# Linear attention and a gated MLP on one core: 512-token chunks with a chunk of tails, block-diagonal kv, 1 KB loads, crossbar transposes of q, and a hand-made order

## The chip, the cores and the metric

The kernel runs on one core of a Trainium2 chip. The metric is the device time of one execution in microseconds (us); lower is better. The profile is one execution recorded by the hardware profiler. Its span runs from the first to the last recorded instruction and is a few us shorter than the timed execution. Engines are named as the profile names them: PE (matrix multiplier), PEld (its weight loads, which overlap PE), DVE (vector engine), ACT (activation engine), POOL (general engine), SP (here only the issuer of DMAs).

## The reference

Eight batches, eight heads, 576 tokens, head size 64. All inputs are float32.

```python
q_s = exp(q) / sum(exp(q), over the 64 features)    # the reference also subtracts maxima first
k_s = exp(k) / sum(exp(k), over the 576 tokens)
kv  = k_s^T v                    # 64 x 64 for each batch and head
x   = q_s kv                     # (8*576 = 4608 tokens) x 512, heads side by side
h   = x @ w_in                   # 512 -> 2048
g   = h * sigmoid(beta * h)
out = g @ w_out                  # 2048 -> 512
```

Both kernels use bfloat16 operands for the matmuls, leave the maxima out (the inputs are small), and get the sum over tokens for k from a column of ones appended to v. The MLP is the bulk: for each 512 tokens it takes 128 matmuls of 128x512 (64 into h, 64 into the output). For 4608 tokens that makes 1152.

## The kernel before

Tokens are cut in nine chunks of 512. A batch has 576 tokens, so each batch falls into two chunks, and into four blocks of 128 rows and one of 64. A scheduler chooses the order of instructions. The parts that matter, with cuts marked by `...`:

```python
S_CHUNKS = [(0, 128), (128, 128), (256, 128), (384, 128), (512, 64)]
...
qt = stage.tile([P, H, D], F32, tag="q_st", bufs=NSC)
nc.sync.dma_start(qt[:rows], q[b, :, s0 : s0 + rows, :].rearrange("h p d -> p h d"))     # 256 B runs
...
vt = atn.tile([P, H, D + 1], BF16, tag="vaug", bufs=ATN_DEEP)
nc.gpsimd.dma_start(vt[:rows, :, 0:D], v[b, ...])          # the DMA casts float32 to bfloat16
...
nc.vector.memset(vaug[ci][:rows, :, D : D + 1], 1.0)       # column of ones, again in every batch
...
for j in range(HP):                                        # two heads at a time
    for ci, (s0, rows) in enumerate(S_CHUNKS):             # four blocks of 128 rows, one of 64
        nc.tensor.matmul(kvE[:, :], Ek[ci][:rows, ds(P * j, P)], vaug[ci][:rows]..., ...)
    ...
    for ci, (s0, rows) in enumerate(S_CHUNKS):
        nc.tensor.transpose(qsT_ps[:, s0 : s0 + rows], qs[ci][:rows]..., identity[:rows, :rows])
    ...
    # x: two 64x64 matmuls side by side, one head each
    nc.tensor.matmul(xps[0:D, 0:w], kvp[0:D, :], qsT[0:D, ...], tile_position=(0, 0))
    nc.tensor.matmul(xps[D:P, 0:w], kvp[D:P, :], qsT[D:P, ...], tile_position=(64, 64))
    nc.scalar.copy(xT[c][:, j, off : off + w], xps[:, 0:w])
```

The MLP comes in two passes per chunk: all of h and g (`mlp_A`), then the output (`mlp_B`, one chunk behind).

The softmax here doesn't subtract the row's maximum and nothing guards it: scores larger than these inputs give would overflow.

## Time and profile before

| | before |
|---|---|
| time, first three runs | 370.23 us median (369.5 to 370.23) |
| span of the profiled run | 366.7 us |
| first MLP weight load starts at | 34.2 us |
| 129th (a chunk's worth later) | 87.5 us |
| 257th | 123.2 us |
| 1152nd, the last | 362.1 us |

The weight loads of the MLP's matmuls are a good ruler: there are exactly 1152 in both kernels, so the n-th one marks the same progress, whatever the order. Back to back, 128 of the matmuls take 27.6 us (0.2157 us from one start to the next), so a chunk cannot be shorter than that.

First, the page of the kernel before: its span, PE's busy line, and three rows in 40 slices of the span (granted PE clock in tenths of full speed, DMA share in tenths, GB/s).

```profile
span 366.7 us, 4552 instructions
...
PE 317.5 (87%) x1570; PEld 139.3 (38%) x1600; DVE 207.0 (56%) x477; ACT 185.2 (50%) x325; POOL 69.3 (19%) x86
...
PEclk9999768999999999999999999999999999999999
DMA  8999999649719802950293019001001000100111
GB/s 187 250 356 327 266 254 241 160 103 219 204 46 188 221 31 78 182 150 27 62 179 115 2 57 93 30 0 57 27 3 57 32 29 2 57 29 29 59 67 76
```

PE is busy 87% of the time. In the first seven slices (64 us) the DMA engines are nearly full, but move only 187 to 356 GB/s. The granted clock is known only from the first clock record of a trace on, at 37.8 us in the kernel before; the views count the time ahead of it as full speed. Next, PE's waits over the whole run, with the instruction that ended each (total us, times, longest us).

```profile
PE qsT_ps L179 <- DVE qst L137: 17.8, 5, 9.8
PE hT L213 <- DVE g L225: 12.9, 11, 3.4
PE kvE L157 <- DVE vt L127: 7.2, 3, 3.3
```

The first line is mostly the start: q has to be loaded, exponentiated and normalized before it can be transposed. The third is the ones column: `vt L127` is the memset. The stretches view gives for each stretch its length, the busy time of PE, PEld, DVE, ACT and POOL with counts, then the granted clock, the DMA share (the summed times of all packets over 16 engines, so it can exceed 1), and GB/s.

```profile
34.20:87.50 53.30, 44.36 (x203) 17.84 (x206) 38.21 (x94) 31.22 (x60) 18.68 (x22) 0.87 1.15 205
...
160.80:198.30 37.50, 35.50 (x182) 15.68 (x185) 23.83 (x57) 21.20 (x39) 8.44 (x10) 1.00 0.51 93
```

The first chunk's worth of MLP work took 53.3 us, a later one 37.5 us, in which PE counts as busy for 35.5. In the first, the granted clock fell twice to one half for 6.8 us, and 27 of the 128 MLP matmuls took about 0.63 us each instead of 0.38. Busy isn't the same as useful: the timeline of PE shows how a 64-row block sits among the others (start, us, engine, line, operation, operands, size of the weights, size of the result).

```profile
251.94 0.39 PE L157 MATMUL kvE<-vt,Ekt 128*128 128x130 bf16 x4
252.26 0.24 PE L193 MATMUL xps<-qsT,kvp 64*64 64x128 bf16 x1
252.26 0.24 PE L199 MATMUL xps<-qsT,kvp 64*64 64x128 bf16 x1
252.43 0.23 PE L157 MATMUL kvE<-vt,Ekt 64*128 64x130 bf16 x1
252.59 0.40 PE L179 MATMUL qsT_ps<-identity,qst 128*128 128x128 bf16 x4
```

From the start of the 64x64 pair to that of the 64x128 matmul it is 0.17 us, and 0.16 us more until the next 128x128 one may start. Matmuls of this size and equal tiles start 0.057 us apart in the same trace. The Trainium skill, "TensorEngine Tiling (Array Packing)", "Key Properties", says: "Changing tiling mode (not just tile) drains the TensorE". The trace agrees, and shows the price.

### The profile page before, as it was taken

How to read it: one execution, taken by the hardware profiler on the slowest of the kernel's cores; microseconds unless marked ns; L12 is line 12 of the kernel's file. 1: busy time of each engine (PE TensorE's matmuls, PEld its weight loads, DVE VectorE, ACT ScalarE, POOL GpSimd, SP SyncE). 2: the span in 40 equal slices, each digit the busy share in tenths (PEclk: the TensorE clock that was granted, in tenths of full speed). 3: DMA queues.
4: the chain of work that ended last, by engine and by line, in shares of the span. 5: the costliest groups of instructions: out<-in, count | busy, mean ns of one | idle time of the engine just before them, and what ended most of it. 6: DMA issues, size and time to landing. Idle time of an engine off the chain costs nothing.

```text
span 366.7 us, 4552 instructions
## 1 busy us (share of the span) xinstructions
PE 317.5 (87%) x1570; PEld 139.3 (38%) x1600; DVE 207.0 (56%) x477; ACT 185.2 (50%) x325; POOL 69.3 (19%) x86
## 2 busy tenths in 40 slices
PE   0125669899998999899989998999999999999995
PEld 0011223443433444344433443345344444444442
DVE  1554736988988937664767566654452545255100
ACT  3312426768668745755485538552554355355211
POOL 8281433035017001800090004000000000000000
PEclk9999768999999999999999999999999999999999
DMA  8999999649719802950293019001001000100111
GB/s 187 250 356 327 266 254 241 160 103 219 204 46 188 221 31 78 182 150 27 62 179 115 2 57 93 30 0 57 27 3 57 32 29 2 57 29 29 59 67 76
DMA packets 88486, 41.72 MB, mean 114 GB/s; under 512 B 78480, under 2 KB 78480, under 8 KB 88464
## 3 DMA queue, kind: packets, MB, share of 16 engines
q0 software_dynamic: 40448, 14.16, 28.8%
q1 hardware_dynamic: 48016, 27.28, 26.3%
q8 instruction: 12, 0.20, 0.2%
q14 instruction: 10, 0.08, 0.1%
HBM read 36.71 MB, written 9.44 MB: 126 GB/s over the span
## 4 chain that ended last, share of the span: by engine, by line
PE 67%; DMA 12%; DVE 11%; issue 4%; ACT 3%; SPq 2%; POOL 1%; ACTq 0%; POOLq 0%
PE hT L213 30%; PE acc L241 27%; DMA qt<-in_q_dram 6%; DMA vt<-in_v_dram 4%; PE kvE L157 4%; PE qsT_ps L179 3%; DVE g L225 3%; PE xps L193 3%; DMA w_in_st_311<-in_moe_w_in_dram 3%; DVE qst L137 2%; SPq L109 2%; DVE qz L131 2%; ACT th L221 1%; DVE w_in_b L86 1%; DVE qsT L185 1%
## 5 line engine op out<-in xcount | busy, mean ns | idle before, releaser
L241 PE MATMUL acc<-w_out_b,g 128*128 128x512 bf16 x561 | 143.8, 381 | 0.6 <-DVE g L225 0.2
L221 ACT ACTIVATE th<-hT,beta_half 128x512 bf16<-128x512 f32 x144 | 97.8, 686 | 72.4 <-PE hT L213 68.8
L225 DVE SCALAR_TENSOR_TENSOR g<-th,hT 128x512 bf16<-128x512 bf16 x144 | 97.7, 685 | 64.8 <-ACT th L221 64.4
L213 PEld LDWEIGHTS <-w_in_b 128*128 128x128 bf16 x576 | 54.4, 98 | 87.3 <-issue 34.4
L241 PEld LDWEIGHTS <-g 128*128 128x128 bf16 x576 | 54.9, 98 | 63.8 <-issue 0.9
L121 POOL DMA_DIRECT2D vt<-in_v_dram x40 | 33.9, 871 | 121.6 <-DVE qz L131 101.8
L249 ACT COPY o_sb<-acc 128x512 f32<-128x512 f32 x36 | 21.0, 584 | 44.6 <-PE acc L241 41.1
L179 PE MATMUL qsT_ps<-identity,qst 128*128 128x128 bf16 (+1 forms) x160 | 18.8, 226 | 19.1 <-DVE qst L137 17.8
L131 DVE TENSOR_REDUCE qz<-Eq 128x8 f32<-128x512 bf16 (+1 forms) x40 | 26.8, 671 | 13.3 <-ACT Eq L129 8.7
L129 ACT ACTIVATE Eq<-qt 128x512 bf16<-128x512 f32 (+1 forms) x40 | 25.0, 627 | 11.0 <-DMA qt<-in_q_dram 8.5
L137 DVE TENSOR_TENSOR qst<-Eq,rqz 128x512 bf16<-128x512 bf16 (+1 forms) x40 | 27.1, 684 | 2.6 <-DVE rqz L135 1.9
L157 PE MATMUL kvE<-vt,Ekt 128*128 128x130 bf16 (+1 forms) x160 | 20.9, 232 | 7.8 <-DVE vt L127 7.2
L213 PE MATMUL hT<-xT_93,w_in_b 128*128 128x512 bf16 x63 | 20.7, 469 | 6.0 <-DVE g L225 5.8
L193 PE MATMUL xps<-qsT,kvp 64*64 64x512 bf16 (+7 forms) x64 | 20.2, 316 | 3.9 <-DVE kvp L170 2.6
L179 PEld LDWEIGHTS <-qst 128*128 128x128 bf16 (+1 forms) x160 | 11.1, 99 | 27.3 <-DVE qst L137 19.6
L199 PE MATMUL xps<-qsT,kvp 64*64 64x512 bf16 (+7 forms) x64 | 20.3, 317 | 0.3 <-issue 0.3
L167 DVE RECIPROCAL rkz<-kvE 64x1 f32<-64x1 f32 x32 | 5.0, 158 | 27.3 <-PE kvE L157 26.5
L157 PEld LDWEIGHTS <-Ekt 128*128 128x128 bf16 (+1 forms) x160 | 12.4, 100 | 19.6 <-issue 10.7
L213 PE MATMUL hT<-xT_96,w_in_b 128*128 128x512 bf16 x63 | 16.4, 378 | 2.0 <-DVE g L225 2.0
L213 PE MATMUL hT<-xT_97,w_in_b 128*128 128x512 bf16 x63 | 16.5, 378 | 1.6 <-DVE g L225 1.6
L213 PE MATMUL hT<-xT_94,w_in_b 128*128 128x512 bf16 x62 | 16.4, 380 | 0.9 <-DVE g L225 0.8
L213 PE MATMUL hT<-xT_95,w_in_b 128*128 128x512 bf16 x62 | 16.2, 379 | 1.1 <-DVE g L225 0.9
(121 smaller groups left out, 222.7 us busy)
## 6 DMA issues: line engine op xcount, KB each, us to landing
out_dram<-o_sb SPq DMA_DIRECT2D x36, 256.0 KB, 2.0
qt<-in_q_dram SPq DMA_DIRECT2D x32, 256.0 KB, 5.4
vt<-in_v_dram POOLq DMA_DIRECT2D x32, 128.0 KB, 5.6
qt<-in_q_dram SPq DMA_DIRECT2D x8, 128.0 KB, 6.1
w_out_st_315<-in_moe_w_out_dram SPq DMA_DIRECT2D x1, 1024.0 KB, 12.0
w_out_st_317<-in_moe_w_out_dram SPq DMA_DIRECT2D x1, 1024.0 KB, 14.9
w_out_st_319<-in_moe_w_out_dram SPq DMA_DIRECT2D x1, 1024.0 KB, 10.7
w_out_st_321<-in_moe_w_out_dram SPq DMA_DIRECT2D x1, 1024.0 KB, 11.8
```

The lines of the kernel that those rows point to most:

```text
L121: nc.gpsimd.dma_start(vt[:rows, :, 0:D], v[b, :, s0 : s0 + rows, :].rearrange("h p d -> p h d"))
L129: nc.scalar.activation(Eq[:rows], q_st[ci][:rows], ACTF.Exp)
L131: nc.vector.tensor_reduce(qz[:rows], Eq[:rows], axis=mybir.AxisListType.X, op=ALU.add)
L137: nc.vector.tensor_tensor(qst[:rows], Eq[:rows], rqz[:rows].unsqueeze(2).to_broadcast((rows, H, D)), ALU.mult,)
L157: nc.tensor.matmul(kvE[:, :], Ek[ci][:rows, ds(P * j, P)], vaug[ci][:rows].rearrange("p h e -> p (h e)")[:rows, ds(2 * j * (D + 1), 2 * (D ...
L179: nc.tensor.transpose(qsT_ps[:, s0 : s0 + rows], qs[ci][:rows].rearrange("p h d -> p (h d)")[:rows, ds(j * P, P)], identity[:rows, :rows],)
L193: nc.tensor.matmul(xps[0:D, 0:w], kvp[0:D, :], qsT[0:D, s_done : s_done + w], tile_position=(0, 0),)
L213: nc.tensor.matmul(hT[:, :], w_in_b[:, kt, ds(j * P, P)], xT[c][:, kt, :], start=(kt == 0), stop=(kt == KT - 1),)
L221: nc.scalar.activation(th[:, :], hT[:, :], ACTF.Tanh, scale=beta_half[:, j : j + 1])
L225: nc.vector.scalar_tensor_tensor(out=g[:, :], in0=th[:, :], scalar=1.0, in1=hT[:, :], op0=ALU.add, op1=ALU.mult,)
L241: nc.tensor.matmul(acc[:, :], gts[j][:, ds(st * P, P)], w_out_b[:, j, :], start=(j == 0), stop=(j == NJ - 1),)
L249: nc.scalar.copy(o_sb[:, :], acc[:, :])
```

## The change

Its intent: cut each batch into 512 tokens, which make a chunk on their own, and 64 tails, which make a ninth chunk together (8 x 64 = 512). Give each SBUF partition four consecutive tokens, so that a load has 1 KB runs. Make every matmul a full 128x128 tile: the tails of two batches share 128 rows, with zeros in v where the rows belong to the other batch; kv of two heads is one block-diagonal matrix with zeros off the diagonal. Let the DMA's crossbar transpose q from batch 1 on. Write the ones columns once (as 2.0, which also absorbs the factor one half of the tanh form). Interleave the two MLP passes two units apart, with four accumulators, and fix the order of the instructions by hand. POOL casts most of v and w_out.

The diff, cut to its core (cuts marked by `...`):

```diff
-    S_CHUNKS = [(0, 128), (128, 128), (256, 128), (384, 128), (512, 64)]
+    MAIN = R * P            # 512
+    TAIL = S - MAIN         # 64
...
+    ctx.enter_context(tc.manual_schedule())
...
-            nc.sync.dma_start(
-                qt[:rows], q[b, :, s0 : s0 + rows, :].rearrange("h p d -> p h d")
-            )
+    def main_view(t, b):
+        return t[b, :, 0:MAIN, :].rearrange("h (p i) d -> p h (i d)", i=R)
...
-            nc.gpsimd.dma_start(
-                vt[:rows, :, 0:D], v[b, :, s0 : s0 + rows, :].rearrange("h p d -> p h d")
-            )
...
-            nc.vector.memset(vaug[ci][:rows, :, D : D + 1], 1.0)
+    nc.gpsimd.memset(va[0][:, :, :, D:D1], 2.0)        # once; the same for va[1] and the tails
...
-                nc.tensor.transpose(
-                    qsT_ps[:, s0 : s0 + rows],
...
+        nc.sync.dma_start_transpose(
+            qsT[b][:].rearrange("p i j r -> p (i j) r"),
+            qs[b][:].rearrange("p i h d -> p (i h d)"),
+        )
...
-                nc.tensor.matmul(xps[0:D, 0:w], kvp[0:D, :], qsT[0:D, ...], tile_position=(0, 0))
-                nc.tensor.matmul(xps[D:P, 0:w], kvp[D:P, :], qsT[D:P, ...], tile_position=(64, 64))
+            nc.tensor.matmul(t[:], kvp[:, c, j, :], qsT[c][:, :, j, :])
...
+    WARM = 36
+    for wi in range(WARM):                             # dummy matmuls while the first loads arrive
+        t = ps.tile([P, 512], F32, tag="h", bufs=2, name=f"warm{wi}")
+        nc.tensor.matmul(t[:], warm[:, 0:P], warm[:])
...
+    nc.gpsimd.memset(kvp[:, 1:B], 0.0)                 # after the first chunk's x, in program order
+    nc.gpsimd.memset(vt[:, 1:4], 0.0)
...
+            off = {0: "q0", 1: "q1", 2: "k0", 3: "k1", 5: "qT", 7: "kv0", 9: "kv1"}   # unit of the chunk
```

The last line is the hand-made order of a chunk: in which of its 16 MLP units the exponentials and sums of the next batch's q, its k, the transpose and kv are issued. This is called side work below.

## The prediction

> **What bounds it now.** The span is 366.7 us. The chain of waits is 67% PE, 12% DMA, 11% DVE. In steady state (timeline after 300 us) four 128x512 matmuls take 0.86 us, so the MLP's 1152 cost about 248 us. Attention on PE costs roughly 40 us: transposes about 92 ns each (x160), kv matmuls about 96 ns (x160), the paired x matmuls about 10 us in all. The other 75 us are idle or slow PE. By the stretches table PE is busy 4.0 of the first 30 us (q and k arrive in 256 B packets; the first MLP matmul starts at 34.2 us), and from 30 to 87 us it stalls for weights and loads (waits of PE: transposes on qst 17.8 us, hT on g 12.9 us) at a granted clock of 0.87 to 0.90. After 115 us PE is over 94% busy.
>
> **What the change does.**
> 1. Start. q0, k0, v0 and one weight block (4.4 MB) must land. The 1 KB loads should reach about the 320-350 GB/s that the best slice of before reaches, so the first block lands near 17.5 us; cast (1.3 us, as the 128x2048 DVE cast now), kv norm and x copies follow. First MLP matmul near 21.5 us: 12-13 us saved.
> 2. Chunk 0. All weights and batch 1 (about 15 MB) stream to 46-50 us, while 16 units of 1.73 us need only 28 us of PE. POOL now casts w_out and v (2048 elements); the trace shows no POOL copy, my estimate is 4-5 us each, from the "GPSIMD Engine Reference", section 3.1, of the Trainium skill (2.6 cycles an element). Its page "SBUF — State Buffer", "Who interferes with whom", says a DVE cast of this kind and POOL exclude each other, so some DVE casts will wait: no view of before shows it. Chunk 1 starts near 58 us, with 5-8 us of PE stall.
> 3. Steady chunks 1-6: 27.6 us MLP + 1.9 kv + 0.9 x. Seven batches' PE transposes (12 us) leave. A new loss: in the first four units of each chunk DVE owes two row sums (1.2 us for 1024 elements, scaled from 0.68 for 512), two normalizations (1.2), two output copies (0.6) and four g (0.69): near 10 us against 7 us of PE. With two h buffers and single output accumulators, I expect 2 us of PE stall a chunk: 32.5 us each, 195 us together. The crossbar transpose (512 KB) has about 9 us before x needs it; I expect it hidden.
> 4. Chunk 7 about 31.5 us, chunk 8 about 28 us, drain and last store 5 us.
>
> Sum: 58+195+31.5+28+5 = 318 us span; the timed runs are 3.5 us above the span: 321 us. I shade to 318, as the order was presumably tuned.
>
> **Prediction: 318 us, range 302 to 336.** Faster by over 2%: 0.98; within 2%: 0.015; slower: 0.005. The gain, all on the critical path: 13 us start, 15 us PE transposes and x, 20 us stalls between 34 and 115 us.
>
> **What would show it.** First hT matmul 19-24 us; chunk-1 start 54-63 us; PE's waits, before the first matmul of a chunk's second or third unit, on output copies (accumulators) and on g; no PE wait on the transposed q; DMA mostly over 300 GB/s in the first 40 us.
>
> **What would make it wrong.** A slow crossbar transpose, or one that stops other loads (then x waits in each chunk: up to 5 us x 7); POOL casts much slower than estimated, delaying w_out and v in chunk 0; the 4-byte beta load just ahead of the first weight block; or stalls at chunk starts absent (then about 304 us).

## The result and the profile after

| | before | after |
|---|---|---|
| time, median of 4 runs | 369.88 us (369.5 to 370.23) | 316.22 us (314.24 to 316.92) |
| ratio | | 0.8546 (95%: 0.8513 to 0.858) |
| span, profiled run | 366.7 us | 314.3 us |
| mean granted clock (time without a record counted as full) | 0.980 | 0.975 |

A ratio is the mean time of one kernel's runs over the mean of the other's in the same rounds, so it is not quite the ratio of the medians quoted. Executions over 1.5% slower than the fastest of the same kernel are left out of the means. Where two variants are compared that ran in different rounds, I divide their ratios to the kernel before, and multiply by 316.22 us to get microseconds against the changed kernel.

The same parts of the page, after:

```profile
span 314.3 us, 3735 instructions
...
PE 281.7 (90%) x1401; PEld 131.0 (42%) x1428; DVE 189.2 (60%) x292; ACT 153.9 (49%) x220; POOL 40.8 (13%) x41
...
PEclk9958999999999999999999999999999999999996
DMA  7989999995903692379039923870380033012005
GB/s 247 188 295 372 307 347 260 308 285 102 349 18 133 151 293 92 133 166 304 0 134 189 261 88 136 232 235 2 133 184 19 0 146 55 2 42 91 2 0 133
```

PE's waits after, and then two of its stretches:

```profile
PE kv_0_246 L218 <- DVE va_73 L147: 6.2, 1, 6.2
PE tp_2_226 L201 <- DVE qs_207 L182: 3.3, 1, 3.3
...
PE kv_0_515 L218 <- POOL va_74 L147: 1.1, 1, 1.1
...
PE acc_1_1213 L291 <- DVE o_1190 L250: 0.7, 1, 0.7
```

```profile
26.40:62.30 35.90, 31.04 (x148) 13.72 (x152) 22.54 (x34) 17.06 (x25) 8.39 (x5) 1.00 1.08 316
...
125.50:156.20 30.70, 29.80 (x151) 14.01 (x153) 19.55 (x32) 17.21 (x26) 2.10 (x2) 1.00 0.51 154
```

The longest waits for loads and for g are gone. What stays are waits in the start (6.2 and 3.3 us), single ones of up to 1.6 us in the first two chunks, and 0.7 us at the start of each later chunk. In the first chunk the DMA moves 316 GB/s where it moved 205. A later chunk takes 30.7 us instead of 37.5. And the timeline of PE shows kv, tails included, as full tiles that start 0.055 to 0.06 us apart:

```profile
55.23 0.39 PE L218 MATMUL kv_0_515<-va_74,ek_485 128*128 128x130 bf16 x4 [1.09 <-POOL va_74 L147]
55.45 0.22 PE L225 MATMUL kv_0_515<-vt,ekt 128*128 128x130 bf16 x1
55.51 0.39 PE L218 MATMUL kv_0_515<-va_74,ek_485 128*128 128x130 bf16 x4
```

By the ruler of MLP weight loads, the 52.4 us of span divide so:

| stretch | before | after | gain |
|---|---|---|---|
| until the first load | 34.2 | 26.4 | 7.8 |
| 1st to 129th | 53.3 | 35.9 | 17.4 |
| 129th to 257th | 35.7 | 32.5 | 3.2 |
| 257th to the last | 238.9 | 211.0 | 27.9 |
| from the last to the end | 4.6 | 8.5 | -3.9 |

So there are two things to explain: some 28 us in the first chunks, and some 28 us in the steady part. The latter isn't spread evenly: from the 257th load on, the seven pieces of 128 loads (127 in the last) gained 6.9, 6.8, 6.5, 4.5, 4.3, -0.8 and -0.2 us. For the first three of these pieces I took the time that PE spends on each kind of matmul, from the start of each matmul to that of the next. The figure for waits is what remains of the period.

| us for one chunk | before | after |
|---|---|---|
| MLP matmuls, back to back | 27.6 | 27.6 |
| kv | 2.0 | 1.1 |
| transposes of q | 2.1 | 0 |
| x | 2.4 | 0.9 |
| all other waits of PE | 3.4 | 1.1 |
| period | 37.5 | 30.7 |

Of the 6.8 us, 4.5 to 4.6 are matmuls that became cheaper or left, and 2.2 to 2.3 are waits. In the next two pieces PE of the kernel before waits only 0.2 us in all, so the gain there, 4.5 and 4.3 us, can't come from shorter waits. That is bookkeeping; whether each part would have been a gain alone, the experiments tell.

### The profile page after: what moved, and what is told of

It reads as the page before. It is cut to its first block, busy times and chain, and to the rows that moved or that the text cites. A ratio compares the mean times of both kernels' runs of the same rounds, so it can differ in the third digit from the quotient of the medians.

```text
span 314.3 us, 3735 instructions
## 1 busy us (share of the span) xinstructions
PE 281.7 (90%) x1401; PEld 131.0 (42%) x1428; DVE 189.2 (60%) x292; ACT 153.9 (49%) x220; POOL 40.8 (13%) x41
## 4 chain that ended last, share of the span: by engine, by line
PE 71%; DVE 15%; DMA 4%; ACT 4%; issue 3%; POOL 1%; another core or an unknown queue 1%; DVEq 0%; SPq 0%; ACTq 0%; POOLq 0%
DMA v_st_127<-in_v_dram 4%; DVE va_73 L147 2%; PE acc_1_2625 L291 1%; DVE w_in_b L125 1%; PE acc_3_2363 L291 1%; PE acc_2_2362 L291 1%; PE acc_0_2624 L291 1%; PE acc_2_2626 L291 1%; PE acc_2_1214 L291 1%; PE acc_1_2361 L291 1%; PE acc_1_1790 L291 1%; PE acc_1_1498 L291 1%; PE acc_1_2075 L291 1%; PE acc_3_1215 L291 1%; PE acc_0_2360 L291 1%
## 5 line engine op out<-in xcount | busy, mean ns | idle before, releaser
L343 PEld LDWEIGHTS <-warm 128*128 128x128 bf16 x36 | 3.8, 108 | 6.8 <-issue 2.4
L147 DVE CAST va_73<-v_st_101 128x1024 bf16<-128x1024 f32 x2 | 6.3, 3178 | 0.0
L147 POOL CAST va_73<-v_st_998 128x2048 bf16<-128x2048 f32 x1 | 1.9, 1917 | 32.5 <-DMA v_st_998<-in_v_dram 32.5
L147 POOL CAST va_73<-v_st_1575 128x2048 bf16<-128x2048 f32 x1 | 1.9, 1917 | 32.4 <-DMA v_st_1575<-in_v_dram 32.4
L174 DVE TENSOR_REDUCE rq_204<-eq_202 128x16 f32<-128x1024 bf16 x2 | 2.4, 1214 | 5.6 <-ACT eq_202 L161 5.6
L255 PEld LDWEIGHTS <-kvp 128*128 128x128 bf16 x32 | 3.0, 99 | 5.4 <-DVE kvp L239 2.1
L147 POOL CAST va_74<-v_st_1285 128x2048 bf16<-128x2048 f32 x1 | 1.9, 1918 | 24.3 <-DMA v_st_1285<-in_v_dram 24.3
L147 POOL CAST va_74<-v_st_1862 128x2048 bf16<-128x2048 f32 x1 | 1.9, 1918 | 23.5 <-PE x_2_1978 L255 23.5
L182 DVE TENSOR_TENSOR qs_643<-eq_595,rq_597 128x1024 bf16<-128x1024 bf16 x2 | 4.1, 2072 | 0.0
L131 ACT ACTIVATE ek_238<-k_st_94 128x1024 bf16<-128x1024 f32 x2 | 2.1, 1056 | 3.5 <-DMA k_st_94<-in_k_dram 3.5
L147 POOL CAST va_74<-v_st_708 128x2048 bf16<-128x2048 f32 x1 | 1.9, 1919 | 14.3 <-PE x_2_824 L255 14.3
L147 POOL CAST va_73<-v_st_580 128x2048 bf16<-128x2048 f32 x1 | 1.9, 1917 | 13.4 <-DMA v_st_580<-in_v_dram 13.4
L155 POOL CAST vt<-vt_st_99 64x512 bf16<-64x512 f32 x2 | 2.3, 1152 | 9.8 <-DMA vt_st_99<-in_v_dram 9.7
L161 ACT ACTIVATE eq_202<-q_st_91 128x1024 bf16<-128x1024 f32 x2 | 2.1, 1056 | 2.9 <-DMA q_st_91<-in_q_dram 2.9
L225 PEld LDWEIGHTS <-ekt 128*128 128x128 bf16 x32 | 3.3, 104 | 0.0
L155 POOL CAST vt<-vt_st_577 64x512 bf16<-64x512 f32 x2 | 3.3, 1638 | 0.1
L125 POOL CAST w_out_b<-w_out_117 128x2048 bf16<-128x2048 f32 x1 | 2.1, 2072 | 8.7 <-DMA w_out_117<-in_moe_w_out_dram 8.7
```

Source lines behind the costliest of these rows:

```text
L125: eng.tensor_copy(dst, wst[kind, blk][:])
L131: nc.scalar.activation(ek[b][:, :, s * m : (s + 1) * m, :].rearrange("p i h d -> p h i d"), k_st[b][:, s * m : (s + 1) * m, :].rearrange(" ...
L147: eng.tensor_copy(va[b % 2][:, :, s * m : (s + 1) * m, 0:D].rearrange("p i h d -> p h i d"), v_st[b][:, s * m : (s + 1) * m, :].rearrange( ...
L155: eng.tensor_copy(vt[r, pr, e, :, 0:D], vt_st[pr][r])
L174: nc.vector.tensor_reduce(rq[b][:, 0, :, h], eq[b][:, :, h, :], axis=AX.X, op=ALU.add)
L182: nc.vector.tensor_tensor(qs[b][:, :, h, :], eq[b][:, :, h, :], rq[b][:, 1, :, h].unsqueeze(3).to_broadcast((P, R, m, D)), ALU.mult,)
```

## The experiments

Theory at the outset: the steady part gains because PE does less (no transposes, no switches of tile size), and the early part gains because the loads are faster. The rivals: the hand-made order makes most of the gain; or the dummy matmuls keep the clock up; or the crossbar transposes are the main thing. Seven runs undo or move one part of the changed kernel, three put parts of the change into the kernel before, and two try to beat both.

### The steady part, from the changed kernel

**The crossbar.** All transposes back on PE, with DVE copying the results out:

```diff
-XBAR = True
+XBAR = False
```

> Undoes the crossbar: q of batches 1 to 7 and of the tails is transposed on PE again (16 transposes and four DVE copies of 0.42 us a batch). Theory A (the gain is mostly stalls removed by order and loads): transposes go at about 55 ns each in the changed kernel (four from 10.91 to 11.13 us), so 8 x 16 x 55 ns = 7 us more PE work, total +5 to +9 us (about 322 us). Theory B (the gain is PE work removed, as before spent 92 ns on each): +12 us or more (328 us or more). If PE had slack: under +2 us.

Measured: 321.02 us median (319.88 to 323.25), ratio 0.8678, so 0.8678/0.8546 = 1.015, or 4.9 us more. A steady chunk took 31.6 us instead of 30.7. Six of the seven batches fall after the 257th weight load, and that stretch grew by 5.4 us, from 211.0 to 216.4 (6 x 0.9). The crossbar is worth about 5 us, not the 12 us that the prediction charged for seven batches of PE transposes. With full tiles a transpose on PE is cheap. The crossbar itself is hidden. Its line in the changed kernel's timeline is:

```profile
165.52 1.95 SPq L191 DMA_TRANSPOSE qsT_1550<-qs_1505  x1
```

The view of that source line gives 4.3, 4.4 and 9.4 us (least, median, most) from issue to landing for 512 KB, the longest in the first chunk, where the loads are dense. No wait of PE names the transposed q. The Trainium skill, "Advanced Engine Details and Errata", "X-Bar Transpose (TRN2)", calls these transposes as fast as regular DMAs, at 350-400 GB/s. Here 512 KB in 4.4 us is about 120 GB/s (524,288 bytes divided by 4.4 us), counted from issue to landing; the issuing instruction on SP alone took 1.3 to 2.0 us of it after the first chunk, and plain stores of 512 KB took 3.2 us at the median. So for one transpose at a time, plan with the measured 4.4 us and not with the rate; one size can't tell how much of it is a fixed latency.

**Tile switches.** The x matmul of the changed kernel as two 64x64 ones again, on the same data:

```diff
-            nc.tensor.matmul(t[:], kvp[:, c, j, :], qsT[c][:, :, j, :])
+            for e in range(2):
+                r = slice(e * D, (e + 1) * D)
+                nc.tensor.matmul(t[r, :], kvp[r, c, j, r], qsT[c][r, :, j, :], tile_position=(e * D, e * D))
```

> Undoes the block-diagonal kv in the x matmuls of batches 0 to 7: two 64x64 matmuls on opposite quarters of the array, as before, in place of one 128x128. Theory C (a weight load of another tile size is not loaded ahead: in before the array drained at each switch, 149 ns from the last full kv matmul to the 64-row one and 155 ns to the next full one, against 57 ns between equal tiles): about 0.2 us a pair, 32 pairs, total +5 to +8 us, and a gap before and after each pair. Rival (the two quadrants run at once, so they cost what one matmul does): under +1 us.

Measured: 322.06 us (320.71 to 322.6), ratio 0.8734: 2.2%, or 7.0 us, more. The period rose from 30.7 to 31.6 us, 0.9 us for four pairs, 0.22 us for each. PE's timeline of this run shows it:

```profile
144.84 1.03 PE L293 MATMUL acc<-w_out_b,g 128*128 128x512 bf16 x4
145.79 0.40 PE L257 MATMUL x<-qsT,kvp 64*64 64x512 bf16 x2
146.13 1.03 PE L271 MATMUL h<-xT,w_in_b 128*128 128x512 bf16 x4
```

And the same place in the changed kernel:

```profile
146.88 0.38 PE L291 MATMUL acc_3_1215<-w_out_b,g_9_1335 128*128 128x512 bf16 x1
147.10 0.38 PE L255 MATMUL x_1_1385<-qsT_1266,kvp 128*128 128x512 bf16 x1
147.31 1.03 PE L269 MATMUL h_12_1388<-xT_80,w_in_b 128*128 128x512 bf16 x4
```

A full tile with half of its weights zero costs 0.21 us, start to start. The pair, which does half of that tile's multiplications, and in parallel, costs 0.34 us, and about 0.09 us before it (four matmuls from 144.84 at 0.2157 us would end their slots at 145.70). So zeros are cheaper than a switch. The rival, that a pair running in parallel costs the same as one full tile, falls.

**The hand-made order.** The same program with the scheduler's order:

```diff
-    ctx.enter_context(tc.manual_schedule())
```

> Undoes the hand-made order alone: same instructions, the order on each engine is left to the scheduler. Theory A: the order is worth a large part, +10 to +30 us, with PE gaps in the first 100 us and chunk periods above 30.7 us. Rival (the gain is less work and better loads, whatever the order): under +5 us.

Measured: 312.42 us (311.45 to 314.24), ratio 0.8444. That is 3.8 us faster than the changed kernel, where 10 to 30 us slower had been expected. My expectation was refuted, and with it the rival that the order makes the gain. What the change gained, it gained by its structure, and the order that was fixed by hand was even slightly worse than the scheduler's for the same program. By the ruler the scheduler's order is behind at first (385th load at 127.3 us, 125.5 by hand), and its chunks then take 30.5 us, falling to 29.6, against 30.7.

### The early part, from the changed kernel

**POOL and DVE locking each other out.** In the timeline of the changed kernel, all engines, the start looks like this:

```profile
15.17 3.08 POOL L364 MEMSET kvp<- 128x3584 bf16 x1
...
15.93 6.28 DVE L147 CAST va_73<-v_st_101 128x1024 bf16<-128x1024 f32 x2
...
18.25 2.77 POOL L366 MEMSET vt<- 128x3120 bf16 x1
...
22.12 1.23 DVE L125 CAST w_in_b<-w_in_105 128x2048 bf16<-128x2048 f32 x1
```

Two casts of 1024 elements take 6.28 us, where one of 2048 elements takes 1.23 us. They span POOL's two large memsets. The Trainium skill, "SBUF — State Buffer", "Who interferes with whom", says that a DVE cast in its fast mode and a POOL instruction need the same pair of ports, and whichever starts first blocks the other fully. The test moves POOL's memsets to before the first batch's work:

```diff
+    nc.gpsimd.memset(kvp[:, 1:B], 0.0)
+    nc.gpsimd.memset(va[1][:, :, :, D:D1], 2.0)
+    nc.gpsimd.memset(vt[:, 1:4], 0.0)          # and the small ones that follow it
     nc.gpsimd.memset(kvp[:, 0], 0.0)
     for wi in range(WARM):
...
-    nc.gpsimd.memset(kvp[:, 1:B], 0.0)
-    nc.gpsimd.memset(va[1][:, :, :, D:D1], 2.0)
-    nc.gpsimd.memset(vt[:, 1:4], 0.0)
```

> The POOL memsets of kvp, va and vt move ahead of POOL's wait for the v tail. If they are what made the two DVE casts of v take 3.2 us each (15.9 to 22.2 us), the casts fall to about 0.7 us each; if the casts waited for something else, they stay. Then the first MLP matmul comes 1.5 to 5 us earlier (22 to 25 us, limited by the landing of the first weight block near 20.6). Total: if the DMA stream (last load of batch 1 landing at 53 us) sets the start of chunk 1, the total changes by under 1.5 us; if the start sets it, by 4 to 5 us.

Measured: 315.39 us (314.43 to 316.86), ratio 0.8523; against 0.8546 that is no difference that the intervals can tell. The timeline of this run:

```profile
3.71 3.13 POOL L341 MEMSET kvp<- 128x3584 bf16 x1
...
16.80 1.29 DVE L147 CAST va<-v_st 128x1024 bf16<-128x1024 f32 x2
...
21.55 1.23 DVE L125 CAST w_in_b<-w_in 128x2048 bf16<-128x2048 f32 x1 [3.46 <-DMA w_in<-in_moe_w_in_dram]
```

POOL's memsets did hold up the casts: the mean cast went from 3178 to 690 ns. But the first MLP weight load came only 0.5 us sooner (25.9 us), because DVE then waits 3.46 us for the first weight block, which landed at 21.5 us (20.6 in the changed kernel). One wait was hiding another that ended at about the same time. A difference of 0.5 us between two single traces is no gain that counts: in the runs with PE transposes and with 64x64 pairs, which leave the loads and casts of the start as they are, the first load came at 25.7 and 25.0 us.

**The dummy matmuls.**

```diff
-WARM = 36
+WARM = 0
```

> Takes the 36 dummy matmuls away. They end at 10.9 us, PE then idles from 15.5 to 21.7 us and the granted clock falls to 0.5 before the first kv matmul, so theory A: nothing is gained by them, total within 1 us of the changed kernel, clock in the stretch 16 to 26 us unchanged. Rival (they keep PE fast for the start): the eight to ten transposes and the first MLP matmuls run at half clock, +2 us or more.

Measured: 315.0 us (314.64 to 315.64), ratio 0.8539. The dummies are worth nothing that these runs can see. The idea behind them agrees with the Trainium skill, "TensorE: Matmul & The Clock Gate", "Part 1: The HAM clock gate", which says that PE's clock is halved after an idle window of some 3.4 us and that activity releases it. For 16 to 26 us the stretches view gives a granted clock of 0.53 with the dummies and 1.00 without them, but the second is no measurement: the clock records of that trace begin at 24.6 us, and the time ahead of them counts as full. The matmuls tell more. First without the dummies, then with them:

```profile
8.49 1.03 PE L201 MATMUL tp<-identity,qs 128*128 128x128 bf16 x8 [8.49 <-DVE qs L182]
...
20.97 0.64 PE L218 MATMUL kv<-va,ek 128*128 128x130 bf16 x4
```

```profile
10.91 0.39 PE L201 MATMUL tp_0_210<-identity,qs_207 128*128 128x128 bf16 x4
...
22.22 0.64 PE L218 MATMUL kv_0_246<-va_73,ek_238 128*128 128x130 bf16 x4
```

The transposes start 107 ns apart without the dummies and 55 to 56 ns apart right after them. But the dummies end long before the real work starts, PE then stands idle for the 6.2 us shown above, and from the second kv matmul on they start 107 to 111 ns apart in both runs: half speed, as the records with the dummies show (0.5 from 15.2 to 25.4 us). What the dummies had won was lost before it mattered, as I had expected.

**The length of the runs in the loads.** Each main load in four pieces with 256 B runs, to the same places:

```diff
-            eng.dma_start(t[:, s * n : (s + 1) * n, :], main_view(src, b)[:, s * n : (s + 1) * n, :])
+            for i in range(R):
+                eng.dma_start(
+                    t[:, s * n : (s + 1) * n, i * D : (i + 1) * D],
+                    main_view(src, b)[:, s * n : (s + 1) * n, i * D : (i + 1) * D],
+                )
```

> Undoes the 1 KB loads alone: the same tiles and bytes, but each of q, k, v is loaded in pieces whose contiguous run is 256 B. By the packet times (18 ns for 256 B, 47 ns for 1 KB at the median) a batch's three loads need 55% more DMA time: about 14 against 9 us. Theory A: the first MLP matmul comes 4 to 6 us later and chunk 1 starts 6 to 12 us later, later chunks keep 30.7 us as 14 us of loads fit there; total +6 to +12 us. Rival (the loads are hidden behind PE): under +2 us.

Measured: 321.96 us (321.73 to 322.5), ratio 0.87: 1.8%, or 5.7 us, more. The first weight load came at 27.8 us (26.4 with 1 KB), the 129th at 69.1 (62.3), and the later period was 30.7 us, as in the changed kernel. The whole cost is before the second chunk, as expected (part of it can be the clock: 10 MLP matmuls ran at half speed here, none in the changed kernel's trace); the size is just below the range of 6 to 12 us. The run also has four times as many issues on SP for these loads, so 5.7 us is the cost of both. The traces give the reason in packets: one of 256 B takes 18 ns of its DMA engine (median, in the kernel before and in this run), one of 1 KB takes 47 ns (after), which is 14 against 22 bytes in a nanosecond. The Trainium skill, "DMA: Bandwidth & Descriptors", "Why small descriptors are slow (HBM only)", names a fixed cost for each packet, 27% at 256 B; the traces agree in kind, and show more: the same bytes take 1.53 times as long (4 x 18 against 47 ns).

**The cast of v.** The DMA casts v on its way again, in place of casts by POOL and DVE:

```diff
+        if tag == "v_st":
+            vv = v[b, :, 0:MAIN, :].rearrange("h (p i) d -> p h i d", i=R)
+            for i in range(R):
+                nc.gpsimd.dma_start(va[b % 2][:, i, :, 0:D], vv[:, :, i, :])
+            return
...
     def v_cast(b, eng, s=0, n=1):
+        return
```

> Undoes the way v is loaded: four casting DMAs a batch from POOL's queue, 128 B written per packet (32 ns each in before), in place of the 1 KB f32 load and a POOL or DVE cast. DMA time for a batch's v: 4096 x 32 ns / 16 = 8.2 us against 1024 x 47 / 16 = 3 us. Theory A (before's early part was held by DMA, and v's small packets were its largest item): chunk 1 starts 4 to 10 us later, total +4 to +10 us, later chunks as before at 30.7 us. Rival (v's load is hidden and the cast's POOL and DVE work is saved): between -2 and +2 us.

Measured: three runs of 325.33 to 329.04 us, ratio 0.8884, and one of 362.33 us (granted clock 0.825), which is the profiled one. I count this as inconclusive. It is slower than the changed kernel by 4%, but the only trace shows another cause besides the packets. These lines are from its PE waits (a slow run: read the order, not the sizes), and from its timeline:

```profile
PE acc L297 <- POOL w_out_b L130: 11.7, 1, 11.7
```

```profile
36.85 0.24 POOL L371 MEMSET va<- 128x32 bf16 x1 [17.69 <-DMA va<-in_v_dram]
```

POOL's small memset of ones into the second `va` tile now waits for the load of v into that tile, because both write it. POOL stood there for 17.69 us, with the casts of w_out queued behind, and PE waited for those. The edit changed two things at once; it does not isolate the casting DMA. What the trace of before does show of it: a packet of the casting DMA leaves 128 B, takes 32 ns, and for v alone there are 36864 of them, 74.5 us of each of the 16 engines over the run (about 36864 x 32 ns / 16).

### Parts of the change in the kernel before

**Full tiles only.** Zero-padded tails of 128 rows and a block-diagonal kv in the kernel before; nothing else. The core of the edit:

```diff
+    tail_v = [const.tile([P, H, D + 1], BF16, name=f"tail_v{i}") for i in range(2)]
+    kv_bd = [const.tile([P, P], BF16, name=f"kv_bd{i}") for i in range(2 * HP)]
+    for t in tail_e + tail_v + tail_q + kv_bd:
+        nc.gpsimd.memset(t[:], 0.0)
...
-                    Ek[ci][:rows, ds(P * j, P)],
+                    Ek[ci][:, ds(P * j, P)],
...
-                    identity[:rows, :rows],
+                    identity[:],
...
-                nc.tensor.matmul(xps[0:D, 0:w], ..., tile_position=(0, 0))
-                nc.tensor.matmul(xps[D:P, 0:w], ..., tile_position=(64, 64))
+                nc.tensor.matmul(xps[:, 0:w], kv_bd[...], qsT[:, s_done : s_done + w])
```

> The kernel before, with one part of the change alone: the 64-row tail slices are padded with zeros to 128 rows for the kv matmuls and transposes, and kv is block-diagonal, so all PE tiles are 128x128. Loads, order, scheduler and chunks stay. Theory C (tile-size switches drain PE): about 3.5 us less a batch of PE time, where PE binds: 342 to 352 us. Rival (what the change gained came from loads and order alone): over 363 us.

Measured: 373.71 us (370.36 to 374.53), ratio 1.0111 (1.006 to 1.0163). Slower by 1.1%, where 342 to 352 us had been expected: the clearest miss. The edit did what it should on PE. Attention's matmuls fell from about 6.5 to 3.6 us a chunk. But three steady chunks, between the 257th and the 641st weight load, took 113.3 us (131.6 to 244.9) against 112.3 before (123.2 to 235.5). PE gave all of the saved time back, in waits and at a lower clock. The timeline of this run shows one of them, first on DVE, and then, in a separate view, on PE:

```profile
195.91 0.07 DVE L133 MEMSET vt<- 128x8 bf16 x1
198.47 0.07 DVE L133 MEMSET vt<- 128x8 bf16 x1 [1.93 <-DMA vt<-in_v_dram]
198.56 1.28 DVE L220 SCALAR_TENSOR_TENSOR g<-th,hT 128x512 bf16<-128x512 bf16 x2
```

```profile
199.31 1.02 PE L208 MATMUL hT<-xT,w_in_b 128*128 128x512 bf16 x4 [2.13 <-DVE g L220]
```

DVE works its queue in order. The memset of ones must wait for the load of v into the same tile. While it waits, two g behind it wait too, then both h buffers stay full, and PE stops for 2.13 us. This wait exists in the kernel before as well (the line `PE kvE L157 <- DVE vt L127` above is its relative); that PE, slower at attention, met less of it there is my reading. In the three chunks DVE's waits for v rose from 2.7 to 6.5 us, and PE's listed waits from 5.9 to 11.1.

Two of these waits, of 2.0 and 2.1 us, were each followed within 1.5 us by 3.4 us at a granted clock of one half (135.7 to 139.1 and 200.5 to 203.9 us), in which 15 MLP matmuls ran at half speed; the kernel before had none in its three chunks.

In the next two chunks, where the kernel before has hardly any waits left (0.2 us in all), full tiles do gain by themselves: from the 641st to the 897th load 66.7 us instead of 70.1. The early part lost more: the first weight load came at 41.0 us instead of 34.2. POOL's zeroing holds its first DMA issues back to 5.2 us, but that is not shown to be the reason: in a run below, with the zeroing on DVE, the first load still came at 39.5 us.

**Ones written once only.** v goes to ten fixed tiles whose ones columns are set at the start:

```diff
+    vset = [[const.tile([P, H, D + 1], BF16, name=f"vset{i}_{c}") for c in range(NSC)] for i in range(2)]
...
+            nc.vector.memset(vset[i][c][:, :, D : D + 1], 1.0)
...
-            vt = atn.tile([P, H, D + 1], BF16, tag="vaug", bufs=ATN_DEEP)
+            vt = vset[b % 2][ci]
...
-            nc.vector.memset(vaug[ci][:rows, :, D : D + 1], 1.0)
```

> The kernel before, with one part of the change alone: the column of ones beside v is written once at the start, into two fixed sets of v tiles, so that DVE no longer has, in each batch, five memsets that wait for the v load. Theory D (DVE runs in order, so a memset that waits for a late v holds back the g that PE's next hT needs: in the chain at 184 to 189 us the v load is followed by g): PE's wait for g, 12.9 us in all, falls under 5 us and the total to 350 to 362 us. Rival (v itself is late and PE's kv matmuls wait for it in order instead): the wait moves to the kv matmul, total within 4 us of before.

Measured: 373.18 us (372.08 to 377.07), ratio 1.0121 (1.0064 to 1.0179). The steady part did get better. The stretches view of the kernel before, over three chunks (it ends 0.2 us short of the 641st load), and then that of this run, over its own three:

```profile
123.20:235.30 112.10, 105.81 (x543) 47.14 (x552) 70.63 (x169) 63.31 (x114) 21.09 (x25) 1.00 0.50 87
```

```profile
137.50:244.00 106.50, 105.56 (x543) 47.26 (x552) 70.02 (x153) 63.03 (x114) 21.06 (x25) 1.00 0.65 99
```

PE is now busy 105.56 of 106.50 us; its waits in this stretch are only 0.6 us. It cannot go faster without cheaper or fewer matmuls. But the early part lost 14.3 us in the profiled run (257th weight load at 137.5 us, before 123.2), which was the slowest of the four; by the medians it lost about 10 (3.9 us slower in total, with 5.8 us gained here). One load of w_in took 13.04 us where it took 9.27 before. DVE's cast that waits for it stands ahead of kv in DVE's queue, and PE waits behind that (view below). It is not shown why the loads were slower: both kernels issue the same loads at nearly the same times up to 9.7 us, and already in the first 10 us the DMA moved 153 GB/s here and 199 before; the k and v loads of batch 1 come no earlier than before (mostly 20 to 31 us against 18 to 26).

```profile
PE xps L198 <- DVE kvp L175: 11.3, 2, 10.5
```

**Both together**, with the zeroing on DVE instead of POOL; the edit is the sum of the two above.

> Full 128x128 tiles (as in the run that padded the tails in before) and the ones written once, with the zeroing on DVE instead of POOL so that POOL's first loads are not held up. Theory C+D (padding saved about 3 us of PE a batch but the waits took it back): with the memsets gone the chunk period falls from 37.6 to 33-35 us and the total to 338 to 352 us. Rival (the loads through two buffers still bind): over 362 us.

Measured: 363.85 us (361.91 to 367.13), ratio 0.9859 (0.9802 to 0.9916). The steady period was 34.0 to 34.9 us, against 33 to 35 expected; three chunks took 103.1 us. The total missed its range of 338 to 352 us, since the early part was still slow (first weight load at 39.5 us, 257th at 129.2). For three chunks the four cases are:

| three steady chunks | ones again in each batch | ones once |
|---|---|---|
| 64-row and 64x64 tiles | 112.3 | 106.5 |
| full tiles | 113.3 | 103.1 |

Here full tiles alone gain nothing, ones alone 5.8 us, both 9.2 us: two limits side by side, where taking one away shows the other. In the two chunks that follow, the same four cases took 70.1 and 70.1, 66.7 and 66.7 us: where no late v holds DVE back, the ones are worth nothing, and full tiles 1.7 us a chunk. The change takes both limits away, and its three chunks take 92.1 us. Of the remaining 11.0 us (3.7 a chunk), 0.9 a chunk is the crossbar by the first experiment; the rest, from the interleaved MLP passes, larger DVE instructions, and loads and casts that don't block, I did not separate.

### Versions to beat both

Two bundles put together what the runs had shown: no dummies, memsets early, and beta loaded as 16 rows of 512 B and transposed on PE (the changed kernel loads it in 2048 pieces of 4 B just ahead of the first weight block). One has the scheduler's order; the other keeps the hand-made order, with the side work for q and k two units later, so that it doesn't collide with the output copies at the start of a chunk. The collision, in the changed kernel's timeline:

```profile
128.64 0.68 DVE L250 COPY o_1190<-acc_1_921 128x512 f32<-128x512 f32 x1
...
129.37 0.38 PE L291 MATMUL acc_1_1213<-w_out_b,g_0_1166 128*128 128x512 bf16 x1 [0.73 <-DVE o_1190 L250]
```

```diff
-WARM = 36
+WARM = 0
...
+    nc.sync.dma_start(beta_r[:], moe_beta.rearrange("(j p) -> j p", p=P))
-    nc.sync.dma_start(beta_t[:], moe_beta.rearrange("(j p) -> p j", p=P))
...
+    bt = ps.tile([P, NJ], F32, tag="att", bufs=2, name="bt")
+    nc.tensor.transpose(bt[:], beta_r[:], ident_f[:])
+    nc.vector.tensor_copy(beta_t[:], bt[:])
...                                            # memsets early, as above
                                               # only with the scheduler's order:
-    ctx.enter_context(tc.manual_schedule())
                                               # only with the hand-made order:
-            off = {0: "q0", 1: "q1", 2: "k0", 3: "k1", 5: "qT", 7: "kv0", 9: "kv1"}
+            off = {2: "q0", 3: "q1", 4: "k0", 5: "k1", 6: "qT", 7: "kv0", 9: "kv1"}
-        if c > 0 and u in (2, 3):
-            q_mul(b, u - 2)
+        if c > 0 and u in (4, 5):
+            q_mul(b, u - 4)
```

The scheduler's order:

> The changed kernel with the scheduler's order, no dummies, the POOL memsets before POOL's wait, and beta loaded as 16 rows of 512 B (transposed on PE) in place of 2048 pieces of 4 B just before the first weight block. DMA moved only 231 and 126 GB/s in 8-12 and 12-16 us against 344 in 4-8 us; if beta's small pieces are the cause, the first weight block lands 2-3 us earlier, the first MLP matmul comes at 21-23 us and chunk 1 starts about 3 us earlier: 308 to 311 us. If they are not: 311 to 314 us, as with the scheduler's order alone.

Measured: 312.23 us (310.34 to 313.39, six runs), ratio 0.8448. Its first weight load is the earliest of all, at 20.8 us, but PE waits 8.7 us in 12 places for g, and it ends where the scheduler's order ended without the repairs.

The hand-made order:

> The changed kernel with the hand-made order, no dummies, early memsets, beta as 16 rows, and the q and k work of a chunk started two units later, clear of the copies of the output accumulators. In the changed kernel PE waits 0.7 us for the copy of accumulator 1 in each chunk (5 us in all), because DVE runs a row sum and a g before that copy. If that is right, the wait goes and the chunk period falls from 30.7 to about 29.9 us: total 306 to 311 us. If PE only meets the next wait, the period stays at 30.7 us and the total at 312 to 315 us.

Measured: 307.12 us (306.72 to 310.57, six runs), ratio 0.8332 (0.8291 to 0.8374). This beats both kernels: 17% off the kernel before, and 0.8332/0.8546 = 0.975, or 2.5% off the changed one (not measured in the same rounds, but the intervals lie apart). First weight load at 22.9 us (26.4), steady period 30.1 us (30.7). Its waits show where the 0.6 us went:

```profile
PE acc L293 <- DVE o L252: 1.3, 8, 0.2
```

In the changed kernel this wait was 0.7 us in each chunk. Between 12 and 16 us the DMA moved 315 GB/s, where it had moved 126. The early memsets alone and the missing dummies alone had left the first load at 25.9 and 25.2 us, which is no clear change (25.0 to 26.4 us without either). So the earlier start came with beta's load, which took 1.7 us to land instead of 7.3, or from all three together; beta alone was not run.

With these repairs in both, the hand-made order wins by 5.1 us over the scheduler's. By the ruler it does so in the first three chunks, where PE waits 7.9 us for g in the scheduler's version: the 385th load comes at 118.6 us against 125.3. From there to the last load the scheduler's order is the faster one, 175.5 us against 177.4. Moving the side work is what brought the hand-made period down by 0.6 us, as the early memsets alone and the missing dummies alone had left it at 30.7 us; it is not shown that it makes the lead over the scheduler.

## Why the prediction was right or wrong

The total was right: 318 us predicted, 316.22 measured. It was right partly because errors cancelled.

1. **Start: wrong.** "First hT matmul 19-24 us"; it came at 26.8 us (its weights at 26.4). The step that failed was "the first block lands near 17.5 us; cast (1.3 us ...), kv norm and x copies follow". The block landed at about 20.6 us, not 17.5: between 8 and 16 us the DMA moved only 231 and then 126 GB/s, not 320 to 350. And the two v casts took 6.28 us, locked out by POOL's memsets. The prediction had named the lock, but looked for it in chunk 0, and had named the 4-byte load as a risk. The run with early memsets shows that taking the lock away alone gains nothing clear (25.9 us, where untouched starts vary from 25.0 to 26.4), since the block binds next; both had to go.
2. **Chunk 0 and the first stalls: right.** "Chunk 1 starts near 58 us", range 54 to 63; measured 60.5 us. The first two chunks gained 20.6 us (17.4 + 3.2), where "20 us stalls between 34 and 115 us" had been predicted; how much of it was stalls and how much the clock, no run separates. Two terms in it were off: POOL's cast of 2048 elements was charged at 4 to 5 us and took 1.9 to 2.1 (the 2.6 cycles belong to an instruction with two inputs, as that section of the page says further down; a cast has one). DMA "mostly over 300 GB/s in the first 40 us" was true for only some slices (247, 188, 295, 372, 307).
3. **Steady chunks: mechanism right in part, size wrong.** 32.5 us predicted, 30.7 measured. Mis-sized terms: kv at 1.9 us a chunk (measured 1.1), because the prediction charged the kernel before's average of 96 ns for each matmul, and that average contained the tile switches; with equal tiles it is 57 ns. PE stalls at 2 us (1.1 measured in all, 0.7 of it the predicted wait of an accumulator for its output copy). The predicted wait on g at the same place did not appear as a steady wait. The crossbar was hidden, as predicted. "Seven batches' PE transposes (12 us) leave" was right as bookkeeping of the kernel before, but putting them back as full tiles costs 4.9 us.
4. **What the prediction did not see at all.** It described the steady part before as "PE is over 94% busy", and charged attention's matmuls at their average of 92 and 96 ns, as if all of that were work. Part of it was switching between tile sizes (64-row blocks, 64x64 pairs), and behind that lay a second limit, the ones memset in DVE's queue. The four cases in the kernel before show both. The steady gain was 27.9 us for the last 895 weight loads, where "15 us PE transposes and x" had been counted. Of the 20.2 us in its first three chunks, the two limits account for 9.2 and the crossbar for 2.7; the other 8.3 were not separated.
5. **End: wrong in size.** "Drain and last store 5 us"; it took 8.5. The last chunk holds the tails of eight batches, so its output goes out in eight small stores issued one after another on SP, as the timeline shows; a remedy was not tried.

```profile
306.42 5.05 SPq L307 DMA_DIRECT2D out_dram<-o_2809  x8
```

Added up: chunk 1 began 2.5 us later than predicted, the end took 3.5 us more, and chunk 7 took about 29.7 us where 31.5 had been predicted. Chunks 1 to 6 took 187.6 us by what remains of the span (314.3 less 60.5, 29.7, about 28 for the last chunk, and 8.5), against 195 predicted. So losses of 6.0 us stood against gains of 9.2. The words "hand-made order" in the change were taken as a reason to shade the prediction from 321 to 318 us ("as the order was presumably tuned"); the run with the scheduler's order shows that this was no reason.

What stays open: how the first chunk's 17.4 us divide among 1 KB loads (with the extra issues 5.7 us, measured in the changed kernel), the missing casting DMAs, the weights in larger blocks with POOL sharing the casts, and PE's clock. For the clock I estimate at most 5.7 us: 27 MLP matmuls of the first chunk ran at half speed before, and none in the changed kernel's trace; back to back, such matmuls start 0.43 us apart instead of 0.22 (in the last version's trace, at 23 to 26 us). That trace may be a lucky one: of the fast traces of its variants, seven had 8 to 18 such matmuls in that chunk, and one had none. The run meant for the casting DMA was confounded.

## What to carry to other kernels

A busy engine isn't an engine at work: compare the start-to-start time of the small matmuls with that of equal tiles, and pad with zeros when tile sizes alternate. When an engine works its queue in order, an instruction that waits for a load (here a memset of ones into the loaded tile) holds back everything behind it; write such constants once, in tiles that keep them. Where two limits lie side by side, each removed alone can show nothing or a loss, so test them together before throwing either out, and look in the trace for what the next wait is. Before reading a granted clock from a view, look whether the trace has clock records there; the start-to-start time of equal matmuls is the check.

## What the Trainium skill lacked or had wrong

- "TensorEngine Tiling (Array Packing)", "Key Properties": it says that a change of tiling mode drains PE, but gives no cost. Here a 64-row matmul among 128-row ones took about 160 ns start to start instead of 57 ns, and replacing one full tile by a pair of 64x64 tiles cost 0.22 us more.
- "GPSIMD Engine Reference", 3.1: its 2.6 cycles for each element, behind the prediction's estimate of 4 to 5 us for a cast of 2048 elements in each partition, are tied further down in that section to a two-input `tensor_tensor`, and it names no figure for a cast; the casts took 1.92 us (2.07 for w_out).
- "DMA: Bandwidth & Descriptors", "Why small descriptors are slow (HBM only)": it gives an overhead of 27% at 256 B; here the same bytes took 1.53 times as long in packets of 256 B (18 ns) as in packets of 1 KB (47 ns). No figure was found there for a DMA that casts: 32 ns for a packet that leaves 128 B.
- "Advanced Engine Details and Errata", "X-Bar Transpose (TRN2)": it gives a rate, but no latency for one transpose; 512 KB took 4.3 to 4.4 us, and 9.4 us beside dense loads.
- "TensorE: Matmul & The Clock Gate", Part 1: its account of the clock fits these runs (107 ns between equal matmuls without the dummies or after the idle 6.2 us, 56 ns right after the dummies). What I found on no page is that a trace can lack clock records at its start (24.6 us without the dummies), where the views print full speed.
